# Attention over a cached window beside an MLP, one token: the value rows loaded in longer runs, and the product with them laid out anew

## The chip, the cores and the metric

The kernel runs on one core of one Trainium2 chip. The metric is the device time of one execution in microseconds (us). Before the change it is 99.78 us, the median of 3 runs from 99.64 to 99.85. A core has five engines with an instruction queue each: TensorE (PE, matrix products; its weight loads are listed as PEld), VectorE (DVE), ScalarE (ACT), GpSimd (POOL) and SyncE (SP), which here issues the loads. The loads of one queue are carried out by 16 DMA engines in the order in which they were issued.

## The reference

One token `x` of 1024 numbers is normalised to `xn`; an attention over the last 4096 cached keys and values and an MLP both start from `xn`, and their results are added to `x`:

```python
xn  = layernorm(x)
# A: 32 query heads of 128; 4 groups of keys and values, 8 heads on each; the last W = 4096 rows of 65536
q   = xn @ wq                                   # wq 1024 x 4096
p   = softmax(q . k[:, -W:] * 128 ** -0.5)
o   = p . v[:, -W:]
A   = o.reshape(4096) @ wo                      # wo 4096 x 1024
# B
h   = gelu(layernorm(xn) @ w1 + b1)             # w1 1024 x 3584
B   = h @ w2 + b2                               # w2 3584 x 1024
out = x + A + B
```

Everything is bf16. With one token there is no reuse: each of `wq`, `w1`, `w2`, `wo` and the two cache windows is read once, 39.86 MB in all.

## The kernel before

The kernel is a list of operations in the order of the source. Each `op(engine, ...)` names the tiles that it reads and writes; a small planner (`Plan.emit`) keeps the order of each engine as it is written and puts in the semaphore waits. So the order on an engine, and the order of the loads on SP's queue, are set by hand.

The loads go into four 4-MB buffers `slot[0]` to `slot[3]`, each used several times; a load into a slot waits for the last readers of what was there. In the order of SP's queue: the first row of `wq` (slot 1), the keys K (slot 0), the rest of `wq` (slots 1 and 2), the small biases, `w1` in two halves (slot 1, then slot 0), the values V (slot 2, once the second half of `wq` has been used), the first 14 rows of `w2` in two loads of 6 and 8 rows (slot 3, once the keys have been copied out of it), its last 14 rows (slot 1), the first 16 rows of `wo` in two loads (slot 0), and the last 16 in five (slot 2, once V has been used). A "row" of a weight is what each of the 128 partitions holds of it: partition p has 8 of `wq`'s rows, 28 of `w2`'s, 32 of `wo`'s, each 1024 numbers wide for `w2` and `wo`.

The stages that the change and the prediction touch:

- Keys (L341 to L350). K is loaded in runs of 32 KB: partition 4r + g holds 128 consecutive tokens of group g. DVE transposes it in blocks of 32 x 32 into slot 3, and ACT and DVE copy the blocks to `kT`.
- Scores (L417 to L431). PE multiplies `qm` with `kT` in 32 products of 512 columns, four at a time side by side, one for each of four token sets R; the four groups g are accumulated into one 128 x 1024 result: row 32R + head.
- Softmax (L433 to L467). Copy to `sc`, maximum, exponentials `e128` on ACT (L457) with their sums, transposed in blocks by DVE into `eTb` (L461). `rs` is one over the sum of a head; `grs` is that times the mask `gmask`, which keeps a head's own group.
- MLP. The first half of `w1`'s product (`w1_part(0)`) follows the scores on PE, the second the maximum. DVE adds the bias (`h_pre`, L471), ACT applies gelu (L473), DVE transposes (`hT`, L475). DVE adds 21 of `w2`'s 28 rows, each weighted with a number of its own per partition, into two running sums (`running`, L489, with L486 for the first of one sum); PE takes the other 7 (`PE_ROWS`).
- V's product (`v_step`, L502). 32 products, a first, fifteen turns of a loop of two, and a last one. Partition p of V holds 32 tokens of each group, as four runs of 8 KB; product c has the exponentials of token c for 32 heads as weights (and 96 surplus columns) and 4 x 128 columns of V, so its result has every head against every group. L518 masks it with `grs`, L520 adds the four groups, L522 rounds to `o_bf`.
- Output (L525 to L577). PE spreads `o_bf` to `o8` (four small products, L241), then takes `PE_ROWS` and `wo`'s rows: 16 one at a time, 8 in pairs (`groups=2`, two products side by side in the array), which DVE adds to its running sum (L557), and the last 8 rows apart, with the running sum summed over the partitions between them (products of `run` with `ones_f`). `res` is rounded by DVE and ACT and stored by two small DMAs.

Which loads the running rows and the products wait for is in their keys (`w200`, `w206`, `w21`, `wo00` and so on). The running sums on DVE stand in two batches, nine rows ahead of L518 and twelve behind L522.

## Time and profile before

| | |
|---|---|
| median of 3 runs | 99.78 us (99.64 to 99.85) |
| the profiled execution | 99.68 us, of which its span is 98.4 us |
| PE busy | 56.0 us, 323 products |
| DVE busy | 73.1 us |
| ACT busy | 30.8 us |
| POOL busy | 9.9 us |
| mean granted clock of TensorE | 0.931 |

The span is the time from the first to the last instruction in the hardware profiler's record; the 1.28 us that the execution takes beside it lie outside what the profile shows. Busy times overlap, since the engines run side by side. A wait is put down to what came last. A load's row gives the size of the load and the time from its issue to its landing, which includes the time that it stands behind earlier loads of its queue.

The costliest groups of instructions touched by the change, from the list of groups:

| line, engine | what | count, busy us |
|---|---|---|
| L489 DVE | a row of `w2` into a running sum | 20, 24.2 |
| L235 PE | rows of `wo` | 48, 9.1 |
| L502 PE | V's product | 32, 11.6 |
| L235 PE | scores | 32, 5.3 |
| L235 PE | `w2`'s rows on PE | 14, 3.2 |
| L475 DVE | transpose of `h_sb` | 1, 1.7 |
| L461 DVE | transpose of the exponentials | 1, 1.2 |
| L457 ACT | exponentials | 1, 1.2 |

### The profile page before, as it was taken

To read this page: it belongs to the slowest core of one execution; us is meant where nothing else is said; L and a number is where in the kernel's file an instruction comes from. 1 tells how busy PE (TensorE), PEld (TensorE's weight loads), DVE (VectorE), ACT (ScalarE), POOL (GpSimd) and SP (SyncE) were. 2 spreads that over 40 slices of the span, in tenths; PEclk is the share of its full clock that TensorE was granted. 3 is DMA by queue.
4 is the path that set the end of the run, shared out by engine and by line. 5 is a ranking of instruction groups with operands and counts; after the bars stand their busy time and mean duration, and the time that the engine had idled before them with its cause. 6 is when DMAs were issued, how large, how long until landed. Compare 5 with 4: busy or idle time off the path is not lost.

```text
span 98.4 us, 951 instructions
## 1 busy us (share of the span) xinstructions
PE 56.0 (57%) x323; PEld 16.0 (16%) x220; DVE 73.1 (74%) x75; ACT 30.8 (31%) x29; POOL 9.9 (10%) x22
## 2 busy tenths in 40 slices
PE   0140400699200699930899547977771839595792
PEld 0040000133000234300212211211210101111130
DVE  0146407999999999999005595999989999999231
ACT  0600000099999899992002193000000000000001
POOL 0626810000000670000000000000000000000000
PEclk9999999999996559999579998599999999999999
DMA  3999979999999899989799999999898999999980
GB/s 60 487 426 453 440 310 470 433 533 426 440 426 403 373 385 513 408 373 513 330 426 426 423 438 430 425 426 480 385 524 343 433 426 433 426 433 406 396 323 1
DMA packets 3084, 39.86 MB, mean 405 GB/s; under 512 B 390, under 2 KB 396, under 8 KB 780
## 3 DMA queue, kind: packets, MB, share of 16 engines
q1 hardware_dynamic: 3034, 39.86, 95.7%
q10 hardware_dynamic: 50, 0.00, 0.0%
HBM read 39.86 MB, written 0.00 MB: 405 GB/s over the span
## 4 chain that ended last, share of the span: by engine, by line
DMA 67%; PE 22%; issue 4%; SPq 2%; DVE 0%
DMA slot<-in_A_wq_dram 29%; DMA slot<-in_A_wo_dram 21%; DMA slot<-in_A_v_cache_dram 17%; PE qo_ps L502 12%; PE acc L376 9%; SPq L221 2%; PE acc L241 1%; DVE res L576 0%; PE acc L235 0%
## 5 line engine op out<-in xcount | busy, mean ns | idle before, releaser
L346 ACT COPY kT<-slot 32x1024 bf16<-32x1024 bf16 (+1 forms) x18 | 23.9, 1327 | 15.9 <-DVE slot L341 15.7
L489 DVE SCALAR_TENSOR_TENSOR run<-slot,hTf,run 128x1024 f32<-128x1024 bf16 x20 | 24.2, 1272 | 0.1
L376 PE MATMUL acc<-slot,xw 128*128 x48 | 15.4, 495 | 13.7 <-DMA slot<-in_A_wq_dram 13.7
L341 DVE STREAM_TRANSPOSE slot<-slot 128x4096 bf16<-128x4096 bf16 x4 | 17.4, 4414 | 3.6 <-DMA slot<-in_A_k_cache_dram 3.6
L502 PE MATMUL qo_ps<-slot,eTb 128*128 (+1 forms) x32 | 11.6, 437 | 4.3 <-issue 2.6
L350 DVE COPY kT<-slot 32x4096 bf16<-32x4096 bf16 x10 | 13.2, 1320 | 0.2
L235 PE MATMUL sc_ps<-slot,o 128*1 128x512 bf16 x48 | 9.1, 378 | 4.3 <-DMA slot<-in_A_wo_dram 4.3
L376 PEld LDWEIGHTS acc<-slot,xw 128*128 x48 | 5.5, 115 | 24.3 <-issue 21.9
L577 ACT CAST res<-acc 33x224 bf16<-33x224 f32 x1 | 0.3, 339 | 20.5 <-PE acc L235 20.5
L235 PE MATMUL sc_ps<-kT,qm 128*32 128x512 bf16 x32 | 5.3, 853 | 0.3 <-DVE qm L423 0.3
L502 PEld LDWEIGHTS qo_ps<-slot,eTb 128*128 (+1 forms) x32 | 3.1, 97 | 12.5 <-issue 9.8
L545 ACT CAST o<-misc 128x32 bf16<-128x32 f32 x1 | 0.2, 186 | 15.0 <-PE misc L241 15.0
L227 PEld LDWEIGHTS <-o 128*1 128x1 bf16 x40 | 2.4, 83 | 13.9 <-issue 13.3
L435 DVE COPY sc<-sc_ps 128x512 f32<-128x512 f32 x1 | 0.7, 691 | 4.9 <-PE sc_ps L235 4.9
L241 PE MATMUL acc<-spread,qm 32*128 32x512 bf16 x4 | 1.6, 498 | 3.7 <-POOL qm L322 3.7
L235 PE MATMUL sc_ps<-slot,hT 128*1 128x512 bf16 x14 | 3.2, 378 | 0.5 <-DMA slot<-in_B_w_dram 0.5
L235 PE MATMUL acc<-slot,yT 128*1 128x448 bf16 x64 | 3.4, 353 | 0.0
L434 ACT COPY sc<-sc_ps 128x512 f32<-128x512 f32 x1 | 0.6, 585 | 8.0 <-PE sc_ps L235 8.0
L241 PE MATMUL qo_ps<-selq,q_sb 128*128 128x4 bf16 x8 | 0.4, 166 | 4.3 <-DVE q_sb L395 4.3
L241 PE MATMUL misc<-x,spread 32*128 32x8 bf16 x4 | 0.3, 168 | 4.4 <-POOL spread L262 4.4
L557 DVE TENSOR_TENSOR run<-sc_ps,run 33x512 f32<-33x512 f32 x2 | 1.3, 678 | 1.8 <-PE sc_ps L235 1.8
L235 PE MATMUL acc<-slot,o 128*1 128x288 bf16 (+1 forms) x32 | 2.2, 272 | 0.7 <-DMA slot<-in_A_wo_dram 0.6
(88 smaller groups left out, 43.6 us busy)
## 6 DMA issues: line engine op xcount, KB each, us to landing
slot<-in_B_w_dram SPq DMA_DIRECT2D x3, 3584.0 KB, 16.7
slot<-in_A_wo_dram SPq DMA_DIRECT2D x3, 2048.0 KB, 23.7
slot<-in_A_k_cache_dram SPq DMA_DIRECT2D x1, 4096.0 KB, 14.0
slot<-in_A_wq_dram SPq DMA_DIRECT2D x1, 4096.0 KB, 28.6
slot<-in_A_v_cache_dram SPq DMA_DIRECT2D x1, 4096.0 KB, 16.8
slot<-in_A_wq_dram SPq DMA_DIRECT2D x2, 1024.0 KB, 9.8
slot<-in_A_wq_dram SPq DMA_DIRECT2D x1, 2048.0 KB, 19.3
slot<-in_B_w_dram SPq DMA_DIRECT2D x1, 2048.0 KB, 21.5
```

Of the source, the lines that this page charges most:

```text
L221: plan.add(eng, lambda: q.dma_start(out=out_ap, in_=in_ap), r, w, True, over)
L227: return pe.add_instruction(mybir.InstLdweights(name=nc.get_next_instruction_name(), engine=i.engine, tile_size=(P, 32), tile_position=pos ...
L235: return pe.add_instruction(mybir.InstMatmult(name=nc.get_next_instruction_name(), engine=i.engine, start_tensor_calc=start, stop_tensor_c ...
L241: op("pe", lambda: pe.matmul(out_ap, lhsT=w_ap, rhs=x_ap, start=start, stop=stop, tile_position=pos), r, w)
L341: op("dve", lambda s=s: dve.transpose(out=scr[:, s, :], in_=k2[:, s, :]), ("k", "slot0"), (f"scr{s}",))
L346: op("act", lambda s0=s0, s1=s1, R=R, Cd=Cd: act.copy(out=kT[32 * Cd:32 * Cd + 32, R, s0:s1, :].rearrange("p s (c j) -> p (s c) j", j=32), ...
L350: op("dve", lambda R=R, Cd=Cd: dve.tensor_copy(out=kT[32 * Cd:32 * Cd + 32, R, :, :].rearrange("p s (c j) -> p (s c) j", j=32), in_=T3[32 ...
L376: pe.matmul(acc2[:, b, :], lhsT=xw[:, bass.ds(32 * n + 512 * i, P)], rhs=slot[1 + i][:, bass.ds(1024 * n + 512 * b, 512)], start=False, st ...
L435: op("dve", lambda: dve.tensor_copy(out=sc[:, 0:512], in_=sc_ps[:, 0, :]), ("sc0",), ("scs0",))
L489: op("dve", lambda: dve.scalar_tensor_tensor(out=t, in0=wap, scalar=hTf[:, c:c + 1], in1=t, op0=ALU.mult, op1=ALU.add), (key, "hTf", f"run ...
L502: return pe.matmul(qo_ps, lhsT=cols, rhs=v4[:, :, c, :], start=first, stop=last)
L557: op("dve", lambda half=half: dve.tensor_tensor(out=run[0][0:33, 512 * half:512 * half + 512], in0=bulk[:, half, :], in1=run[0][0:33, 512 ...
```

## The change

- V is loaded in runs of 32 KB, as K is: partition 4r + g holds 128 consecutive tokens of group g. It goes into slot 3 and waits for the copies of the keys. The first 14 rows of `w2` go into slot 2, in one load instead of two, and are issued ahead of V. The last 16 rows of `wo` go into slot 3, behind V's product.
- The scores' rows are now 32g + 8u + h for group g, one of four tokens u and head h of the group. `qm` is a 128 x 4 x 4 x 32 tile with each group's heads at four places. The number and size of the products stay.
- The exponentials, transposed in blocks, are moved across partitions by two products with a permutation `perm` into PSUM (`e_ps`), so that they lie as V lies. ACT then writes them four times into `eM`, scaled with `own[:, g]`, which is 1 on the partitions that hold group g and 0 elsewhere (`own_heads`). One of the four stands ahead of the gelu on ACT, three behind it.
- V's product still has 32 steps of 512 columns. Step w has the exponentials of four tokens, 4 x 32 heads, as weights and the same four tokens of V as columns; of the 4 x 4 blocks of the result only the diagonal ones are wanted. DVE copies these four blocks out of PSUM and adds them; ACT rounds, and multiplies with `rs`.
- `gmask`, `grs` and the padding of `eTb` go. `perm` and `own` are made on DVE.
- DVE's batches of running rows are 16 ahead of V's blocks and 5 behind. On PE, `PE_ROWS` stand ahead of the spreading of `o_bf`; all 24 rows of `wo` that go through `bulk_rows` are taken in pairs.

```diff
+    e_ps = ps("e_ps", [P, NCH * 4, REP])
...
-    gmask = sb("gmask", [Hq, Hkv], FP32)
...
+    own = sb("own", [P, Hkv], FP32)
+    op("dve", lambda: dve.tensor_reduce(out=own, in_=ident_f.rearrange("p (r g) -> p g r", g=Hkv), axis=AX.X, op=ALU.add), ("ident_f",), ("own",))
+    perm = sb("perm", [P, P], BF16)
+    op("dve", lambda: dve.tensor_copy(out=perm.rearrange("p (r g) -> p r g", g=Hkv), in_=ident_f.rearrange("p (g r) -> p r g", g=Hkv)), ("ident_f",), ("perm",))
-    qm = sb("qm", [P, Hkv, Hq], BF16)
+    qm = sb("qm", [P, Hkv, 4, Hq], BF16)
...
-    dma("sp", v_sb.rearrange("p (g n) -> p g n", g=Hkv), A_v_cache[0, :, Sk - W:Sk, :].rearrange("g (p c) d -> p g (c d)", p=P), (), ("v0",), ("slot2",))
+    w2_t = [slot[i][:, :14 * D].rearrange("p (r n) -> p r n", r=14) for i in (2, 1)]
+    dma("sp", w2_t[0], w2_v[:, 0:14, :], (), ("w20",), ("slot2",))
+    v_sb = slot[3]
...
-    for a, b in ((0, 6), (6, 14)):
-        dma("sp", w2_t[0][:, a:b, :], w2_v[:, a:b, :], (), (f"w20{a}",), kt_srcs)
+    dma("sp", v_sb, A_v_cache[0, :, Sk - W:Sk, :].rearrange("g (r c) d -> r g (c d)", r=P // Hkv), (), ("v0",), kt_srcs)
     dma("sp", w2_t[1], w2_v[:, 14:28, :], (), ("w21",), ("slot1",))
...
+    for b in range(2):
+        mm32(e_ps[:, 64 * b:64 * b + 64, :], perm, eTb[:, 64 * b:64 * b + 64, :], True, True, ("perm", "eTb"), (f"e_ps{b}",))
...
+    eM = sb("eM", [P, NCH * 4, Hq], BF16)
+
+    def own_heads(g):
+        op("act", lambda: act.activation(out=eM[:, :, REP * g:REP * g + REP], in_=e_ps, func=ACT.Copy, scale=own[:, g:g + 1]),
+           ("e_ps0", "e_ps1", "own"), (f"eM{g}",))
...
+    own_heads(0)
     h_sb = sb("h_sb", [P, 2 * NH], BF16)
     op("act", lambda: act.activation(out=h_sb, in_=h_pre.rearrange("p b n -> p (b n)"), func=ACT.Gelu_apprx_tanh), ("h_pre",), ("h_sb",))
+    for g in (1, 2, 3):
+        own_heads(g)
...
-    for c in dve_rows[:9]:
+    for c in dve_rows[:16]:
         running(c)
...
-        cols = eTb[:, bass.ds(32 * c, P)] if not isinstance(c, int) else eTb[:, 32 * c:32 * c + P]
-        return pe.matmul(qo_ps, lhsT=cols, rhs=v4[:, :, c, :], start=first, stop=last)
+            cols, keys = eM_w[:, bass.ds(P * w, P)], v_sb[:, bass.ds(512 * w, 512)]
+        return pe.matmul(qo_ps, lhsT=cols, rhs=keys, start=first, stop=last)
...
-        dma("sp", wo_t[1][:, a:b, :], wo_v[:, 16 + a:16 + b, :], (), (f"wo1{a}",), ("slot2",))
-    o_m = sb("o_m", [Hq, Hkv, Dh], FP32)
-    op("dve", lambda: dve.tensor_tensor(out=o_m, in0=o_all.rearrange("h (g d) -> h g d", g=Hkv), in1=grs.unsqueeze(2).to_broadcast([Hq, Hkv, Dh]), op=ALU.mult), ("qo", "grs"), ("o_m",))
+        dma("sp", wo_t[1][:, a:b, :], wo_v[:, 16 + a:16 + b, :], (), (f"wo1{a}",), ("slot3",))
+    o_u = sb("o_u", [Hq, 4, Dh], FP32)
+    for u in range(4):
+        op("dve", lambda u=u: dve.tensor_copy(out=o_u[:, u, :], in_=qo_ps[32 * u:32 * u + 32, Dh * u:Dh * u + Dh]), ("qo",), (f"o_u{u}",))
...
-    op("dve", lambda: dve.tensor_copy(out=o_bf, in_=o_f), ("o_f",), ("o_bf",))
-    for c in dve_rows[9:]:
+    op("act", lambda: act.activation(out=o_bf, in_=o_f, func=ACT.Copy, scale=rs), ("o_f", "rs"), ("o_bf",))
+    for c in dve_rows[16:]:
         running(c)
...
+    bulk_rows(PE_ROWS, w2_row, hcol, "hT", first=True)
     o8_ps = misc[:, 160:192]
...
-    bulk_rows(PE_ROWS, w2_row, hcol, "hT", first=True)
...
-    bulk_rows(list(range(16)), wo_row, ocol, "o8")
-    bulk_rows(list(range(16, NB)), wo_row, ocol, "o8", last=True, groups=2)
+    bulk_rows(list(range(NB)), wo_row, ocol, "o8", last=True, groups=2)
```

More of the change, by code (lines that the diff above doesn't have):

```diff
@@ L271 @@
                                           pattern=[[32, 4]], channel_multiplier=1), ("selq",), ("selq",))
-    gmask = sb("gmask", [Hq, Hkv], FP32)
-    op("pool", lambda: pool.memset(gmask, 1.0), (), ("gmask",))
-    op("pool", lambda: pool.affine_select(out=gmask, in_=gmask, compare_op=ALU.is_ge, fill=0.0, base=0,
-                                          pattern=[[-REP, Hkv]], channel_multiplier=1), ("gmask",), ("gmask",))
-    op("pool", lambda: pool.affine_select(out=gmask, in_=gmask, compare_op=ALU.is_ge, fill=0.0, base=REP - 1,
-                                          pattern=[[REP, Hkv]], channel_multiplier=-1), ("gmask",), ("gmask",))
     ones_f = sb("ones_f", [P, P], FP32)
@@ L319 @@
     sel4 = sb("sel4", [P, Hq], FP32)
-    op("dve", lambda: dve.tensor_reduce(out=sel4, in_=ident_f.rearrange("p (r h) -> p h r", r=4), axis=AX.X, op=ALU.add), ("ident_f",), ("sel4",))
-    qm = sb("qm", [P, Hkv, Hq], BF16)
+    op("dve", lambda: dve.tensor_reduce(out=sel4.rearrange("p (g h) -> p g h", g=Hkv), in_=ident_f.rearrange("p (g u h) -> p g h u", g=Hkv, u=4),
+                                        axis=AX.X, op=ALU.add), ("ident_f",), ("sel4",))
+    own = sb("own", [P, Hkv], FP32)
[3 more added lines that the diff above has]
+    qm = sb("qm", [P, Hkv, 4, Hq], BF16)
     op("pool", lambda: pool.memset(qm, 0.0), (), ("qm",))
@@ L378, in wq_rows @@
         return rows
-    qz, zrow = qm.rearrange("p g h -> p (g h)")[0:Hq, :], spread.rearrange("p u n -> p (u n)")
+    qz, zrow = qm[0:Hq, 0, :, :].rearrange("p u h -> p (u h)"), spread.rearrange("p u n -> p (u n)")
     for b in range(2):
@@ L398 @@
     dma("sp", w1_t[1], w1_v[:, 4:8, :], (), ("w11",), ("slot0",))
-    v_sb = slot[2]
-    v4 = v_sb.rearrange("p (g c d) -> p g c d", g=Hkv, c=NCH)
-    dma("sp", v_sb.rearrange("p (g n) -> p g n", g=Hkv), A_v_cache[0, :, Sk - W:Sk, :].rearrange("g (p c) d -> p g (c d)", p=P), (), ("v0",), ("slot2",))
+    w2_t = [slot[i][:, :14 * D].rearrange("p (r n) -> p r n", r=14) for i in (2, 1)]
+    dma("sp", w2_t[0], w2_v[:, 0:14, :], (), ("w20",), ("slot2",))
+    v_sb = slot[3]
     def w1_part(i):
@@ L420 @@
             mm32(qT_ps[:, k, :], blk, selq, True, True, (f"q_sb{b}", "selq"), ("qo",))
-    qm_d = qm.rearrange("p g h -> p (g h)")
-    qm_d = bass.AP(tensor=qm_d.tensor, offset=qm_d.offset, ap=[list(qm_d.ap[0]), [Hq + REP, Hkv], [1, REP]])
-    op("dve", lambda: dve.tensor_copy(out=qm_d, in_=qT_ps.rearrange("p k g -> p g k")), ("qo",), ("qm",))
-    for g in range(Hkv):
-        for R in range(4):
-            ldw(qm[:, g, :], (0, 32 * R), ("qm",))
+    qm_d = bass.AP(tensor=qm.tensor, offset=qm.offset, ap=[list(qm.ap[0]), [4 * Hq, Hkv], [Hq + REP, 4], [1, REP]])
+    op("dve", lambda: dve.tensor_copy(out=qm_d, in_=qT_ps.rearrange("p k g -> p g k").unsqueeze(2).to_broadcast([P, Hkv, 4, REP])), ("qo",), ("qm",))
+    for u in range(4):
+        for g in range(Hkv):
+            ldw(qm[:, g, u, :], (0, 32 * g), ("qm",))
         for a in range(2):
-            for R in range(4):
-                kv = kT[:, R, :, :].rearrange("p u (b r h) -> p h b u r", r=8, h=Hkv)[:, g, 16 * a:16 * a + 16]
-                mm(sc_ps[32 * R:32 * R + 32, a, :].rearrange("p (b r u) -> p b u r", r=8, u=4), qm[:, g, :], kv,
-                   g == 0, g == Hkv - 1, (0, 32 * R), kt_keys, (f"sc{a}",))
+            for g in range(Hkv):
+                kv = kT.rearrange("p q s (w u r k) -> p k u (s w) q r", u=4, r=8, k=Hkv)[:, g, u, 16 * a:16 * a + 16, :, :]
+                mm(sc_ps[32 * g:32 * g + 32, a, :].rearrange("p (w q r) -> p w q r", q=4, r=8), qm[:, g, u, :], kv,
+                   u == 0, u == 3, (0, 32 * g), kt_keys, (f"sc{a}",))
     w1_part(0)
@@ L435 @@
     op("dve", lambda: dve.tensor_copy(out=sc[:, 0:512], in_=sc_ps[:, 0, :]), ("sc0",), ("scs0",))
-    w2_t = [slot[i][:, :14 * D].rearrange("p (r n) -> p r n", r=14) for i in (3, 1)]
-    for a, b in ((0, 6), (6, 14)):
-        dma("sp", w2_t[0][:, a:b, :], w2_v[:, a:b, :], (), (f"w20{a}",), kt_srcs)
+    dma("sp", v_sb, A_v_cache[0, :, Sk - W:Sk, :].rearrange("g (r c) d -> r g (c d)", r=P // Hkv), (), ("v0",), kt_srcs)
     dma("sp", w2_t[1], w2_v[:, 14:28, :], (), ("w21",), ("slot1",))
@@ L444 @@
     op("pe", lambda: pe.transpose(mT_ps, m_loc, ident_f), ("m_loc", "ident_f"), ("misc",))
-    m_row = sb("m_row", [1, Hq], FP32)
-    op("dve", lambda: dve.tensor_reduce(out=m_row, in_=mT_ps.rearrange("a (r h) -> a h r", r=4), axis=AX.X, op=ALU.max), ("misc",), ("m_row",))
-    m_rep = sb("m_rep", [1, 4, Hq], FP32)
-    op("dve", lambda: dve.tensor_copy(out=m_rep, in_=m_row.unsqueeze(1).to_broadcast([1, 4, Hq])), ("m_row",), ("m_rep",))
+    m_row = sb("m_row", [1, Hkv, REP], FP32)
+    op("dve", lambda: dve.tensor_reduce(out=m_row, in_=mT_ps.rearrange("a (g u h) -> a g h u", g=Hkv, u=4), axis=AX.X, op=ALU.max), ("misc",), ("m_row",))
+    m_rep = sb("m_rep", [1, Hkv, 4, REP], FP32)
+    op("dve", lambda: dve.tensor_copy(out=m_rep, in_=m_row.unsqueeze(2).to_broadcast([1, Hkv, 4, REP])), ("m_row",), ("m_rep",))
     mc_ps = misc[:, 128:129]
-    mm32(mc_ps, m_rep.rearrange("a r h -> a (r h)"), ones_f[0:1, 0:1], True, True, ("m_rep", "ones_f"), ("misc",))
+    mm32(mc_ps, m_rep.rearrange("a g u h -> a (g u h)"), ones_f[0:1, 0:1], True, True, ("m_rep", "ones_f"), ("misc",))
     w1_part(1)
@@ L458 @@
     op("act", lambda: act.activation(out=dummy[:, 1:2], in_=mhalf[0:1, 0:1], func=ACT.Gelu_apprx_tanh), ("mhalf",), ("act_warm",))
-    eTb = sb("eTb", [P, WQ4 + 96], BF16)
-    op("pool", lambda: pool.memset(eTb[:, WQ4:], 0.0), (), ("eTb_pad",))
-    op("dve", lambda: dve.transpose(out=eTb[:, :WQ4], in_=e128), ("e128",), ("eTb",))
+    eTb = sb("eTb", [P, NCH * 4, REP], BF16)
+    op("dve", lambda: dve.transpose(out=eTb.rearrange("p c h -> p (c h)"), in_=e128), ("e128",), ("eTb",))
+    for b in range(2):
+        mm32(e_ps[:, 64 * b:64 * b + 64, :], perm, eTb[:, 64 * b:64 * b + 64, :], True, True, ("perm", "eTb"), (f"e_ps{b}",))
     rs_ps = misc[0:Hq, 144:145]
@@ L465 @@
     op("dve", lambda: dve.reciprocal(out=rs, in_=rs_ps), ("misc",), ("rs",))
-    grs = sb("grs", [Hq, Hkv], FP32)
-    op("dve", lambda: dve.tensor_scalar_mul(out=grs, in0=gmask, scalar1=rs), ("gmask", "rs"), ("grs",))
+    eM = sb("eM", [P, NCH * 4, Hq], BF16)
+    def own_heads(g):
+        op("act", lambda: act.activation(out=eM[:, :, REP * g:REP * g + REP], in_=e_ps, func=ACT.Copy, scale=own[:, g:g + 1]),
+           ("e_ps0", "e_ps1", "own"), (f"eM{g}",))
     h_pre = sb("h_pre", [P, 2, NH], FP32)
     op("dve", lambda: dve.tensor_tensor(out=h_pre, in0=acc2[:, :, :NH], in1=b1x.rearrange("p (b n) -> p b n", b=2), op=ALU.add), ("acc2", "b1x"), ("h_pre",))
+    own_heads(0)
     h_sb = sb("h_sb", [P, 2 * NH], BF16)
     op("act", lambda: act.activation(out=h_sb, in_=h_pre.rearrange("p b n -> p (b n)"), func=ACT.Gelu_apprx_tanh), ("h_pre",), ("h_sb",))
+    for g in (1, 2, 3):
+        own_heads(g)
     hT = sb("hT", [P, CW2, 32], BF16)
@@ L480, in w2_row @@
         i, r = divmod(c, 14)
-        return w2_t[i][:, r, :], "w21" if i else f"w20{0 if r < 6 else 6}"
+        return w2_t[i][:, r, :], "w21" if i else "w20"
     def running(c):
@@ L492, with v_step @@
     dve_rows = [c for c in range(CW2) if c not in PE_ROWS]
-    for c in dve_rows[:9]:
+    for c in dve_rows[:16]:
         running(c)
-    o_all = qo_ps[0:Hq, :]
-    v_in = ("eTb", "eTb_pad", "v0", "slot2")
-    def v_step(c, first, last):
-        cols = eTb[:, bass.ds(32 * c, P)] if not isinstance(c, int) else eTb[:, 32 * c:32 * c + P]
-        return pe.matmul(qo_ps, lhsT=cols, rhs=v4[:, :, c, :], start=first, stop=last)
+    v_in = ("eM0", "eM1", "eM2", "eM3", "v0", "slot3")
+    eM_w = eM.rearrange("p c h -> p (c h)")
+    def v_step(w, first, last):
+        if isinstance(w, int):
+            cols, keys = eM_w[:, P * w:P * w + P], v_sb[:, 512 * w:512 * w + 512]
+        else:
+            cols, keys = eM_w[:, bass.ds(P * w, P)], v_sb[:, bass.ds(512 * w, 512)]
+        return pe.matmul(qo_ps, lhsT=cols, rhs=keys, start=first, stop=last)
     def v_rows(i):
@@ L510 @@
     op("pe", lambda: v_step(NCH - 1, False, True), v_in, ("qo",))
-    wo_t = [slot[s].rearrange("p (r n) -> p r n", r=16) for s in (0, 2)]
+    wo_t = [slot[s].rearrange("p (r n) -> p r n", r=16) for s in (0, 3)]
     for a in (0, 8):
@@ L515 @@
     for a, b in zip(cuts[:-1], cuts[1:]):
-        dma("sp", wo_t[1][:, a:b, :], wo_v[:, 16 + a:16 + b, :], (), (f"wo1{a}",), ("slot2",))
-    o_m = sb("o_m", [Hq, Hkv, Dh], FP32)
-    op("dve", lambda: dve.tensor_tensor(out=o_m, in0=o_all.rearrange("h (g d) -> h g d", g=Hkv), in1=grs.unsqueeze(2).to_broadcast([Hq, Hkv, Dh]), op=ALU.mult), ("qo", "grs"), ("o_m",))
+        dma("sp", wo_t[1][:, a:b, :], wo_v[:, 16 + a:16 + b, :], (), (f"wo1{a}",), ("slot3",))
+    o_u = sb("o_u", [Hq, 4, Dh], FP32)
+    for u in range(4):
+        op("dve", lambda u=u: dve.tensor_copy(out=o_u[:, u, :], in_=qo_ps[32 * u:32 * u + 32, Dh * u:Dh * u + Dh]), ("qo",), (f"o_u{u}",))
     o_f = sb("o_f", [Hq, Dh], FP32)
-    op("dve", lambda: dve.tensor_reduce(out=o_f, in_=o_m.rearrange("h g d -> h d g"), axis=AX.X, op=ALU.add), ("o_m",), ("o_f",))
+    op("dve", lambda: dve.tensor_reduce(out=o_f, in_=o_u.rearrange("h u d -> h d u"), axis=AX.X, op=ALU.add), ("o_u0", "o_u1", "o_u2", "o_u3"), ("o_f",))
     o_bf = sb("o_bf", [Hq, Dh], BF16)
-    op("dve", lambda: dve.tensor_copy(out=o_bf, in_=o_f), ("o_f",), ("o_bf",))
-    for c in dve_rows[9:]:
+    op("act", lambda: act.activation(out=o_bf, in_=o_f, func=ACT.Copy, scale=rs), ("o_f", "rs"), ("o_bf",))
+    for c in dve_rows[16:]:
         running(c)
```

## The prediction, made before the changed kernel was run

> **What bounds the kernel now.** I read the page's DMA part first, then the rows of the loads one by one, then TensorE's and VectorE's rows in order of time.

> ```profile
> DMA  3999979999999899989799999999898999999980
> DMA packets 3084, 39.86 MB, mean 405 GB/s; under 512 B 390, under 2 KB 396, under 8 KB 780
> q1 hardware_dynamic: 3034, 39.86, 95.7%
> ```

> SP's queue keeps the 16 DMA engines busy 95.7% of the span; only the first slice and the last one and a half are empty. So it is not an engine that sets the time, but how long the packets take, plus a head and a tail. Rows of single loads (KB, us from issue to landing), and below them their issues (start us, us):

> ```profile
> slot<-in_A_wq_dram SPq DMA_DIRECT2D x1, 1024.0 KB, 4.8
> slot<-in_A_k_cache_dram SPq DMA_DIRECT2D x1, 4096.0 KB, 14.0
> slot<-in_B_w_dram SPq DMA_DIRECT2D x1, 3584.0 KB, 16.7
> slot<-in_A_v_cache_dram SPq DMA_DIRECT2D x1, 4096.0 KB, 16.8
> slot<-in_B_w_dram SPq DMA_DIRECT2D x1, 2048.0 KB, 21.5
> ```

> ```profile
> 0.80 0.40 SPq L207 DMA_DIRECT2D slot<-in_A_wq_dram  x1
> 1.26 0.64 SPq L207 DMA_DIRECT2D slot<-in_A_k_cache_dram  x1
> 32.73 0.33 SPq L221 DMA_DIRECT2D slot<-in_B_w_dram  x1
> 42.60 0.38 SPq L221 DMA_DIRECT2D slot<-in_A_v_cache_dram  x1
> 46.46 0.45 SPq L221 DMA_DIRECT2D slot<-in_B_w_dram  x1
> ```

> Issue plus latency is the landing, and a load's own time is its landing less that of the load ahead of it. K, runs of 32 KB: 1.26 + 14.0 = 15.26, behind a first row of wq at 0.80 + 4.8 = 5.6: 9.7 us. V, the same 4 MB in runs of 8 KB: 42.60 + 16.8 = 59.4, behind w1 at 32.73 + 16.7 = 49.4: 9.95 us. The landings in the trace have a digit more: 5.55, 15.25, 49.43, 59.37, so 9.70 and 9.94. The packet records say the same: 311 ns on average for an 8-KB packet of V, 1214 ns for a 32-KB packet of K, that is 30 ns less than four of 8 KB.

> ```profile
> 59.51 1.03 PE L502 MATMUL qo_ps<-slot,eTb 128*128 128x512 bf16 x3 [1.72 <-DMA slot<-in_A_v_cache_dram]
> 72.73 0.94 PE L502 MATMUL qo_ps<-slot,eTb 128*128 x3 [0.26 <-issue]
> 76.51 3.18 PE L235 MATMUL sc_ps<-slot,hT 128*1 128x512 bf16 x14 [0.52 <-DMA slot<-in_B_w_dram]
> 91.18 1.89 PE L235 MATMUL sc_ps<-slot,o 128*1 128x512 bf16 x16 [1.28 <-DMA slot<-in_A_wo_dram]
> 93.67 1.03 PE L235 MATMUL acc<-slot,o 128*1 128x288 bf16 x16 [0.60 <-DMA slot<-in_A_wo_dram]
> 65.00 8.45 DVE L489 SCALAR_TENSOR_TENSOR run<-slot,hTf,run 128x1024 f32<-128x1024 bf16 x7
> 90.05 1.23 DVE L525 TENSOR_TENSOR run<-run 128x1024 f32<-128x1024 f32 x1
> 93.11 1.28 DVE L557 TENSOR_TENSOR run<-sc_ps,run 33x512 f32<-33x512 f32 x2 [1.83 <-PE sc_ps L235]
> ```

> PE waits for a landing ahead of every stage (V, w2's end, wo's pieces), DVE for PE at the end. From w1's landing on, each load lands as soon as its bytes allow. The last lands at 96.23; 2.17 us of products, rounding and stores end the span.

> **The change, part by part.** *V's runs.* 512 packets become 128. K has this very layout (partition 4r + g) and size, so V's load should take 9.70 us in place of 9.94: -0.24. Bounds: nothing, if V keeps its present rate; -0.25 by the packet records (512 x 311 / 16 against 128 x 1214 / 16). I take K's row.

> [...]

> *w2's first 14 rows in one load.* Its two loads landed at 63.06 and 67.96, 8.58 us behind V. The same 3.5 MB as one load of 28-KB runs is w21: 67.96 to 76.46, 8.50. So -0.08 (bounds 0 and -0.08), and SP has one issue fewer.

> *The order on SP.* The load into slot 2 waits as V's did (42.60), the one into slot 3 as w2's did (46.09); no wait is new. The engines start on them at 49 and later, so both are early, and w21's issue, queued behind, still waits for PE until 54.3. V now lands 8.50 later less 0.24: 49.43 + 8.50 + 9.70 = 67.63. w20 lands at 57.93.

> *wo's last 16 rows wait for V's product.* In the rows it runs from 59.51 to 73.69: 14.18 us for 32 steps, and it has 32 steps of 512 columns still, with as many register instructions in the loop. So 67.78 to 81.96. Queued behind V stand w21 and wo's first 16 rows; their packets are through near 85.5 (86.25, the landing now, less 0.32 and less the 0.4 from last packet to landing), and then the DMA engines run dry. First packets follow an issue by 1.0 us (0.80 to 1.82 at the start), so the product may end at 84.5: 2.5 us to spare. Without that cover every us of lateness is a us of the total.

> *Exponentials.* eTb is ready at 58.80. Two permuting products of 512 columns take 0.60 (the pair at L241), the small one of the sums follows at 59.7, the reciprocal queued behind it ends at 59.9, and h_pre, queued behind that on DVE, ends at 61.0 in place of 60.1. A mask of 1024 numbers per partition costs 1.15, by the exponentials' own row (bounds 1.0, from the 512-wide PSUM copy of 0.585, and 1.9, the 2048-wide key copy). The first is over by 60.7, so gelu waits for h_pre alone; three more end at 65.4 (67.7 at 1.9 each): V comes at 67.63. All of this lies under V's load. For qm's copy, four times as wide (0.19 now), I add 0.1; the scores' 32 products, of the same shapes with other strides, I leave at 5.29, and allow 0.5 either way. Running rows so start 1.0 later, at 64.1.

> *DVE.* Its first nine rows took 10.32 us (63.13 to 73.45), a further row 1.204 (8.45 / 7 in the row above, 14.42 / 12 later). Sixteen end at 64.1 + 10.32 + 7 x 1.204 = 82.85, after V's product. Four block copies from PSUM at 0.29 (between 0.19 for 32 columns and 0.69 for 512) and the sum, 1.00: 85.0. Five rows, 6.02, and L525's add, 1.23: 92.25 in place of 91.28. It is needed when the bulk products end, at 93.1 less what the loads gain, 92.8: 0.55 to spare, the thinnest margin.

> *PE.* PE_ROWS (3.18) follow V's product at once, to 85.15; o_bf is there at 85.25, o8 at 85.9, and wo's second 8 rows land at 86.25 - 0.32 = 85.93. Sixteen rows in pairs at 1.89 per eight end at 89.7, the next 8 land at 90.8. 1.1 to spare; one at a time (3.61 per eight) they would not fit, so the pairs pay for the later start.

> *Set-up.* own and perm on DVE (under 0.73 each, as sel4's row) fall into its 3.6 us of waiting for K; without that they would cost 1 us. POOL drops gmask's three and makes qm four times as large (+0.3 at most, as spread's 0.51); the products behind it wait for wq until 18.1 anyway.

> Sum: -0.24 - 0.08 = -0.32, all of it in the loads. 99.68 - 0.32 = 99.36 for an execution like the profiled one, which lies 0.10 under the median; for the median, 99.46.

> **The rivals.** *Run length gives nothing in this place:* V at its present rate. For it, the rate from landing to landing hardly changes anywhere (K 4.19 MB in 9.70, V in 9.94 us); against it, three sizes of run stand in order (wq's second half, 32 KB, also takes 9.73, with the small biases among it). 99.7 to 99.8, within 0.2%.

> *DVE comes last.* Place: the add of L525 and the sums behind it. It decides from 0.55 us on. For it, DVE has no gap from 64 to 92, and everything added ahead of h_pre or between the rows lands in that chain. With block copies at the upper row of 0.69 (+1.6) and scores slower by 0.5, it is 2.1 late, 1.55 beyond the margin: 101.0; with half of that 100.0. Against it, the narrow PSUM copy's 0.19 is nearer in size than the wide one.

> *The clock falls to half in the last stage.* PE idles from about 60 to 67.6. These windows show what V's product does then (us, PE busy, clock, DMA share, GB/s):

> ```profile
> 60.85:64.30 3.45, 3.45 (x8) 0.51 1.07 454
> 64.30:73.70 9.40, 7.04 (x22) 1.00 1.03 443
> ```

> Eight steps in 3.45 at half clock, 22 in 9.40 at full: 0.43 us a step both times, so a cold start costs it nothing. The pairs leave idle time at 89.7 to 90.8; should the clock halve for 3.4 us behind that, the last 24 products and the 16 behind them would lose about 1.5: 101.0. Against it, the stretches of 3.4 us from 74.5 and 84.8 were busy for 49% and 62% and the clock stayed at full speed; it fell behind the one from 57.44, at 42%, and mine are never below 60%. [...]

> **How the numbers follow.** The forecast 0.68; run length worthless 0.10; DVE last 0.12; the clock 0.06; anything else late, V's product above all, 0.04. The forecast's own range is 99.3 to 99.65. A measurement tells about 0.2% here, 0.2 us. Faster than 99.58: 0.63, nearly all of the forecast. Within: the rest of it, the first rival, a slight lateness of DVE, 0.18. Slower: 0.19. The range goes from 99.25, a faster median by the spread of the runs, to 100.2, the milder half of the late cases.

> **What would show it.** V's load between landings 9.7 us, w2's first load 8.5; the DMA engines without a gap until the last load, 0.3 earlier; V's product starting at its landing, not at a mask; wo's last rows issued near 82; DVE waiting for PE, if briefly, ahead of the final sums. Wrong would make it: a gap between wo's halves in the DMA slices, PE waiting for DVE ahead of the products of run, or V at 9.9.

## The result, and the profile after

The change makes the kernel slower: 102.84 us, the median of 6 runs from 102.74 to 104.08, against 99.86 (99.64 to 100.68); the ratio is 1.031, with a 95% interval from 1.026 to 1.036. The forecast was 99.46 in a range from 99.25 to 100.2.

But the span became shorter. In the other executions of the changed kernel it is 98.1 to 98.3 us, where the kernel before has 98.3 to 98.7. In the profiled one it is 99.2, since one of the 16 DMA engines fell 0.9 us behind while K was loaded (fifteen of K's 16 parts had landed by 15.26, the last at 16.15), and the loads behind it wait for it as well (fifteen parts of V by 67.63, the last at 68.49). What grew is the part of the execution beside the span: 1.28 us before (99.68 - 98.40), 4.6 to 5.0 now (102.79 - 98.2 and its like). Here is the DMA view of the changed kernel from 98.5 to 106 us, in 40 slices of 0.19 us:

```profile
DMA  0000000000000000040000000000000000000000
q8 instruction: 1, 0.02, 1.1%
```

and the same view of the kernel before from 98 us on:

```profile
DMA packets 0, 0.00 MB, mean 0 GB/s; under 512 B 0, under 2 KB 0, under 8 KB 0
```

2.6 us after the last instruction of the changed kernel has ended, at slice 17 (101.7 us), one packet of 16 KB is loaded that isn't data but instructions. It takes 1.37 us by its record. If the 104.08 us of this execution are counted from the start of the span, it ends 1.0 us behind the packet. The page shows nothing of it: it stops at the span.

Within the span, the page's DMA part and the rows of the loads answer to those of before:

```profile
DMA  3999979999999899899899899999899999999960
q1 hardware_dynamic: 2506, 39.86, 95.1%
slot<-in_B_w_dram SPq DMA_DIRECT2D x1, 3584.0 KB, 16.6
33.63 0.33 SPq L222 DMA_DIRECT2D slot<-in_B_w_dram  x1
slot<-in_B_w_dram SPq DMA_DIRECT2D x1, 3584.0 KB, 15.3
43.43 0.33 SPq L222 DMA_DIRECT2D slot<-in_B_w_dram  x1
slot<-in_A_v_cache_dram SPq DMA_DIRECT2D x1, 4096.0 KB, 21.5
46.95 0.59 SPq L222 DMA_DIRECT2D slot<-in_A_v_cache_dram  x1
```

w1's second half lands at 50.2, w2's first 14 rows at 58.7, V at 68.5. In the trace's digits: 50.27, 58.78, 68.49, so 8.51 us for w2's rows (8.58 before) and 9.72 for V (9.94). The DMA engines have no gap until the end. TensorE and VectorE, in order of time:

```profile
68.63 6.62 PE L506 MATMUL qo_ps<-slot,eM 128*128 128x512 bf16 x15 [9.41 <-DMA slot<-in_A_v_cache_dram]
81.89 0.89 PE L506 MATMUL qo_ps<-slot,eM 128*128 x3 [0.30 <-issue]
86.37 3.62 PE L236 MATMUL sc_ps<-slot,o 128*1 128x512 bf16 x32 [0.28 <-ACT o L551]
92.02 1.89 PE L236 MATMUL sc_ps<-slot,o 128*1 128x512 bf16 x16 [2.04 <-DMA slot<-in_A_wo_dram]
82.82 1.18 DVE L523 COPY o_u<-qo_ps 32x128 f32<-32x128 f32 x4 [0.75 <-PE qo_ps L506]
91.07 1.23 DVE L530 TENSOR_TENSOR run<-run 128x1024 f32<-128x1024 f32 x1
93.95 1.28 DVE L560 TENSOR_TENSOR run<-sc_ps,run 33x512 f32<-33x512 f32 x2 [1.66 <-PE sc_ps L236]
```

V's product starts at V's landing, wo's pairs wait 2.0 us for their last rows, and VectorE waits 1.7 us ahead of the final sums. Everything that the prediction hid is hidden. The loss is all outside the span.

### The profile page after: what moved, and what is told of

Same layout as the page of the kernel before. It is cut to its first block, busy times and chain, and to the rows that moved or that the text cites. A ratio compares the mean times of both kernels' runs of the same rounds, so it can differ in the third digit from the quotient of the medians.

```text
span 99.2 us, 956 instructions
## 1 busy us (share of the span) xinstructions
PE 51.4 (52%) x324; PEld 15.0 (15%) x222; DVE 74.6 (75%) x78; ACT 35.3 (36%) x34; POOL 8.7 (9%) x18
## 2 busy tenths in 40 slices
DMA packets 2556, 39.86 MB, mean 402 GB/s; under 512 B 374, under 2 KB 380, under 8 KB 764
## 3 DMA queue, kind: packets, MB, share of 16 engines
q1 hardware_dynamic: 2506, 39.86, 95.1%
HBM read 39.86 MB, written 0.00 MB: 402 GB/s over the span
## 4 chain that ended last, share of the span: by engine, by line
DMA 48%; DVE 31%; PE 15%; issue 3%; SPq 1%
DMA slot<-in_A_v_cache_dram 22%; DVE slot L340 18%; DMA slot<-in_A_k_cache_dram 15%; DVE kT L349 13%; PE qo_ps L506 12%; DMA slot<-in_A_wo_dram 11%; PE acc L236 2%; PE acc L242 1%; DVE res L579 0%; SPq L208 0%; SPq L222 0%
## 5 line engine op out<-in xcount | busy, mean ns | idle before, releaser
L345 ACT COPY kT<-slot 32x1024 bf16<-32x1024 bf16 (+1 forms) x18 | 23.9, 1327 | 16.8 <-DVE slot L340 16.6
L506 PE MATMUL qo_ps<-slot,eM 128*128 (+1 forms) x32 | 12.0, 480 | 11.6 <-DMA slot<-in_A_v_cache_dram 9.4
L236 PE MATMUL sc_ps<-slot,o 128*1 128x512 bf16 x48 | 5.5, 378 | 2.3 <-DMA slot<-in_A_wo_dram 2.0
L506 PEld LDWEIGHTS qo_ps<-slot,eM 128*128 (+1 forms) x32 | 3.2, 99 | 20.2 <-issue 18.1
L465 ACT ACTIVATE eM<-e_ps,own 128x1024 bf16<-128x1024 f32 x4 | 4.2, 1108 | 0.5 <-PE e_ps L242 0.5
L236 PE MATMUL sc_ps<-kT,qm 128*32 128x512 bf16 x32 | 3.9, 647 | 0.4 <-DVE qm L420 0.4
L228 PEld LDWEIGHTS <-o 128*1 128x1 bf16 x40 | 1.7, 83 | 8.4 <-issue 7.3
L311 DVE TENSOR_SCALAR yT<-xn,st 128x8 bf16<-128x8 f32 x1 | 2.1, 2135 | 0.7 <-POOL st L309 0.7
## 6 DMA issues: line engine op xcount, KB each, us to landing
slot<-in_B_w_dram SPq DMA_DIRECT2D x4, 3584.0 KB, 16.2
slot<-in_A_wo_dram SPq DMA_DIRECT2D x3, 2048.0 KB, 24.7
slot<-in_A_k_cache_dram SPq DMA_DIRECT2D x1, 4096.0 KB, 14.9
slot<-in_A_wq_dram SPq DMA_DIRECT2D x1, 4096.0 KB, 29.5
slot<-in_A_v_cache_dram SPq DMA_DIRECT2D x1, 4096.0 KB, 21.5
slot<-in_A_wq_dram SPq DMA_DIRECT2D x2, 1024.0 KB, 10.2
slot<-in_A_wq_dram SPq DMA_DIRECT2D x1, 2048.0 KB, 20.2
slot<-in_A_wo_dram SPq DMA_DIRECT2D x1, 1024.0 KB, 11.3
```

The source lines that it names most:

```text
L228: return pe.add_instruction(mybir.InstLdweights(name=nc.get_next_instruction_name(), engine=i.engine, tile_size=(P, 32), tile_position=pos ...
L236: return pe.add_instruction(mybir.InstMatmult(name=nc.get_next_instruction_name(), engine=i.engine, start_tensor_calc=start, stop_tensor_c ...
L311: op("dve", lambda: dve.tensor_scalar(out=yT, in0=xn, scalar1=st12[:, 2:3], scalar2=st12[:, 6:7], op0=ALU.subtract, op1=ALU.mult), ("xn", ...
L345: op("act", lambda s0=s0, s1=s1, R=R, Cd=Cd: act.copy(out=kT[32 * Cd:32 * Cd + 32, R, s0:s1, :].rearrange("p s (c j) -> p (s c) j", j=32), ...
L465: op("act", lambda: act.activation(out=eM[:, :, REP * g:REP * g + REP], in_=e_ps, func=ACT.Copy, scale=own[:, g:g + 1]), ("e_ps0", "e_ps1" ...
L506: return pe.matmul(qo_ps, lhsT=cols, rhs=keys, start=first, stop=last)
```

## The experiments

What could bring such a fetch is the length of the programs, that is, the number of an engine's instructions, a loop's counted once. TensorE's has 451 instructions before and 455 after: the two permuting products, each with its weight load. ScalarE's went from 53 to 58, VectorE's from 104 to 106, GpSimd's and SyncE's got shorter. All times below are medians beside runs of the kernel before on the same chip; "outside" is the time less the span, as the median over the runs.

**Four instructions more on TensorE alone, or seven on the others.**

```diff
+    for b in range(2):
+        mm32(acc2[:, b, :], qz, zrow, False, False, ("qm", "spread"), ("acc2",))
```

> The kernel before, with two products of zeros more on TensorE at the start (two weight loads and two products, 451 to 455 instructions in TensorE's program, as in the changed kernel); the other engines' programs as before, and TensorE waits for wq there anyway. Theory 'length of TensorE's program': the loss of the change lies outside the span, in a fetch of 16 KB of instructions after the last one, because the program got four instructions longer; this kernel then takes about 103.1 (99.8 + 3.3) with its span at 98.4 as before. Rival 'something in the change's work': 99.8. Rival 'ScalarE's or VectorE's program': 99.8.

103.03 against 99.82, ratio 1.033 (1.029 to 1.038), span 98.55 as before. The profile, from 98.2 us on, shows the packet again, at 100.4 us:

```profile
q8 instruction: 1, 0.02, 0.9%
```

On the other engines (the first line five times, the second twice):

```diff
+    op("act", lambda: act.activation(out=dummy[:, 0:1], in_=mhalf[0:1, 0:1], func=ACT.Exp), ("mhalf",), ("act_warm",))
+    op("dve", lambda: dve.memset(ones_f, 1.0), (), ("ones_f",))
```

> The kernel before, with five tiny activations more on ScalarE and two memsets more on VectorE at the start (53 to 58 and 104 to 106 instructions, as in the changed kernel), TensorE's program unchanged at 451. Theory 'length of TensorE's program': 99.8, span 98.4. Rival 'ScalarE's or VectorE's program': about 103.1.

99.84 against 99.82, ratio 1.000 (0.996 to 1.004), no such packet. The whole loss of the change comes with four instructions on TensorE that do nothing, so it is neither the change's work nor the other engines' programs.

**Two and three more.** One product of zeros as above (453), and with it `ldw(xw[:, 96:97], (0, 0), ("xw",))` (454).

> The kernel before with one product of zeros more on TensorE at the start: 453 instructions in its program, between 451 (nothing fetched at the end) and 455 (3.2 us lost). Theory 'a block boundary in TensorE's program': all or nothing, 99.8 or about 103.1, by whether the end has crossed the boundary, which this run brackets. Rival 'each instruction more costs': about 101.4.

> The kernel before with one product of zeros and one weight load more: 454 instructions on TensorE, between 453 (no fetch) and 455 (3.2 us lost). Theory 'a block boundary': all or nothing, 99.8 or about 103.

453: 99.81 against 99.77, outside 1.31, no packet. 454: 100.15 against 99.74, ratio 1.006 (1.002 to 1.011), outside 1.66 against 1.31, no packet in the record. So neither a cost for each instruction nor quite all or nothing: 0, 0.35, 3.2 us at 453, 454, 455. Where the 0.35 come from isn't settled.

**The change with two and four instructions less.** The maximum of the scores is kept in bf16 (453), then the first sum of x goes through a bf16 product too (451):

```diff
-    m_loc = sb("m_loc", [P, 1], FP32)
+    m_loc = sb("m_loc", [P, 1], BF16)
...
-    op("pe", lambda: pe.transpose(mT_ps, m_loc, ident_f), ("m_loc", "ident_f"), ("misc",))
+    mm32(mT_ps, m_loc, perm, True, True, ("m_loc", "perm"), ("misc",))
...
-    m_rep = sb("m_rep", [1, Hkv, 4, REP], FP32)
+    m_rep = sb("m_rep", [1, Hkv, 4, REP], BF16)
...
-    mm32(mc_ps, m_rep.rearrange("a g u h -> a (g u h)"), ones_f[0:1, 0:1], True, True, ("m_rep", "ones_f"), ("misc",))
+    mm32(mc_ps, m_rep.rearrange("a g u h -> a (g u h)"), spread[0:1, 0, 0:1], True, True, ("m_rep", "spread"), ("misc",))
...
-    mm32(tot, ones_f, st[:, 0:1], True, True, ("ones_f", "st0"), ("misc",))
+    mm32(tot, ones_b, sum_b, True, True, ("ones_b", "st0"), ("misc",))
```

> The changed kernel with the scores' maximum kept in bf16, which makes one fp32 product into a bf16 one and saves two instructions: 453 in TensorE's program. The same work otherwise, and a maximum that is rounded alike in exponent and sum changes nothing in the softmax. Theory 'a block boundary': the same answer as the kernel before at 453, so 99.6 if that took 99.8, or 102.9 if that took 103.1. Rival 'something in the change's work': 102.8 whatever the other does.

> As the one ahead, and the first sum of x through a bf16 product as well, two instructions less: 451 in TensorE's program, as many as the kernel before has. All loads, masks, V's product and wo's pairs as in the changed kernel. Theory 'a block boundary': no fetch at the end, 99.55 (99.8 less 0.25 of the shorter span), faster than both kernels. Rival 'something in the change's work': 102.8.

453: 99.55 against 99.77, ratio 0.9966 (0.9940 to 0.9993). 451: 99.54, ratio 0.9971 (0.9939 to 1.0004). Spans 98.2, outside 1.3 in both, no packet of 16 KB. With all of the change's loads, masks and products in it, the version of 453 is faster than both kernels, by what the prediction saw in the loads or a little less; that of 451 is faster by as much, though its interval just takes in 1.

**448 instructions, in two ways.** First the loop over the second half of wq with one unit a turn:

```diff
-    op("pe", lambda: pe_loop("wq1", 8, wq_rows(1, 2)), ("xw", "wq4", "slot2"), ("acc2",))
+    op("pe", lambda: pe_loop("wq1", 16, wq_rows(1, 1)), ("xw", "wq4", "slot2"), ("acc2",))
```

> The changed kernel with the loop over the second half of wq taking one unit a turn, 16 turns, instead of two a turn, 8 turns: the same products, TensorE's program 448 instructions instead of 455. Theory 'length of TensorE's program': the 3.3 us outside the span go, 99.6, if the longer loop (some 3 us more by the first loop's 0.77 a turn against 1.16) stays hidden behind the copies of the keys; span 98.2 or a little more. Rival 'something in the change's work': 102.8 or more.

100.22 (99.44 to 100.69) against 99.82, ratio 1.003 (0.999 to 1.007), outside 1.26. The 3.3 us are gone, but the spans scatter from 98.2 to 99.4, and a 16-KB packet is there, at 98.24, just before the last instruction ends at 98.27. Then 448 without that loop, the version of 451 with `PE_ROWS = list(range(22, 28))`:

> The changed kernel at 451 instructions, with one of w2's rows moved from TensorE to VectorE: 448 in TensorE's program, without the loop of 16 turns of the other kernel of 448 (100.2 us, with a fetch just at the end of its span). If a length of 448 brings the fetch, it is there again; if the 16 turns brought it, there is none and the time is 99.55, or up to 0.6 more if VectorE's row of 1.2 us no longer fits ahead of the final sums (it had 0.55 to spare by the prediction, 1.0 to 1.6 by the profiles).

99.58 against 99.74, ratio 0.998 (0.995 to 1.001), no packet. The short length isn't what brings the early packet; why the kernel of 16 turns has it stays open.

**The branch hints out, and a program much longer.**

```diff
-            back = self.engines[e].mark_branch_hint_location()
...
-            self.engines[e].br_eq(never[e], 1, f"{e}_main", f"{e}_last").branch_hint(back)
+            self.engines[e].br_eq(never[e], 1, f"{e}_main", f"{e}_last")
```

> The changed kernel with the branch hints of VectorE and TensorE taken out, which name the branch that stands at the end of both programs and its target at their start; 454 instructions on TensorE. If the hints decide which block of instructions is fetched ahead, the block that the end needs is fetched while the program runs: no fetch behind the span, 99.6. If they don't, the fetch stays behind the span: 102.8.

100.97 against 99.77, ratio 1.011 (1.004 to 1.018): outside 1.31, and nothing is fetched behind the span, but the span is 99.65. A 16-KB packet runs at 53.0 us and one of 8 KB at 66.9. Without the hints a packet of 16 KB is fetched at another time. The edit also takes one instruction from TensorE (454); but the kernel before at 454, with its hints, keeps its span (98.45 in the median, 98.4 without the three instructions more), so the hints are the likelier cause, though no run of the changed kernel with 454 instructions and its hints parts the two. The forecast of 99.6 overlooked what a fetch costs in the midst of the loads: w2's first load took 9.77 us instead of 8.51. The same is seen in the kernel before with sixteen products of zeros more (`for b in range(16)`, 483 instructions):

> The kernel before with sixteen products of zeros more on TensorE at the start, under its wait for wq: 483 instructions in its program. If one block boundary near the end is what costs, being 28 instructions further past it than the program of 455 still costs a fetch behind the span, about 3 us: 103. If only a narrow stretch of lengths around 455 is bad, or the block is fetched early enough once the boundary lies well ahead of the end, 99.8 to 101.2.

101.2 against 99.87, ratio 1.011 (1.009 to 1.014); outside 1.31, span 99.8. Its DMA view from 50 to 53 us, and w1's second half and V as loads and as issues:

```profile
q8 instruction: 1, 0.02, 2.2%
slot<-in_B_w_dram SPq DMA_DIRECT2D x1, 3584.0 KB, 16.7
32.75 0.33 SPq L221 DMA_DIRECT2D slot<-in_B_w_dram  x1
slot<-in_A_v_cache_dram SPq DMA_DIRECT2D x1, 4096.0 KB, 18.2
42.51 0.38 SPq L221 DMA_DIRECT2D slot<-in_A_v_cache_dram  x1
```

V lands 11.3 us behind w1 (60.7 less 49.4) instead of 9.94, and all later loads stay as late: the packet, 1.05 us long, goes through one of the 16 engines, each load is shared out over all 16, and the landing waits for the one that was held up. In the trace fifteen of V's 16 parts land from 59.03 to 59.33, the last at 60.75.

Behind the span of the same execution stands a second packet of 16 KB. The DMA view from 98 us on:

```profile
DMA  0000000000000004000000000000000000000000
q8 instruction: 1, 0.02, 1.0%
```

It runs from 101.06 to 102.38, and this execution took 102.08 us, 2.28 beside its span; the other four had 1.23 to 1.31. Counted from the start of the span, the packet ends 0.3 us after the execution. So a packet behind the span doesn't always bring 3.2 us, and here the end did not wait for it.

**V's runs alone,** in the kernel before:

```diff
-    dma("sp", v_sb.rearrange("p (g n) -> p g n", g=Hkv), A_v_cache[0, :, Sk - W:Sk, :].rearrange("g (p c) d -> p g (c d)", p=P), (), ("v0",), ("slot2",))
+    dma("sp", v_sb, A_v_cache[0, :, Sk - W:Sk, :].rearrange("g (r c) d -> r g (c d)", r=P // Hkv), (), ("v0",), ("slot2",))
```

> The kernel before, with V loaded in runs of 32 KB into the same slot at the same place in the queue and nothing else changed, so the tokens that a product meets are not those of its weights and the output isn't the reference's. Theory of the prediction (packet length): V's load 9.70 us between landings instead of 9.94, 99.55 in all, ratio 0.9975. Rival 'run length gives nothing in this place': ratio 1.000.

99.66 against 99.82, ratio 0.9964 (0.9932 to 0.9996); V's load 9.71 us (49.40 to 59.11). The first term of the sum holds as it stands.

**Without the pairs,** the version of 453 with wo's first 16 rows one at a time:

```diff
-    bulk_rows(list(range(NB)), wo_row, ocol, "o8", last=True, groups=2)
+    bulk_rows(list(range(16)), wo_row, ocol, "o8")
+    bulk_rows(list(range(16, NB)), wo_row, ocol, "o8", last=True, groups=2)
```

> The changed kernel at 453 instructions of TensorE, with wo's first 16 rows one at a time as in the kernel before, only the next 8 in pairs. The prediction's step: one at a time they take 7.2 us instead of 3.6 and end at about 92.7, 1.8 after the next rows land at 90.9; the final sums and all behind them come that much later, less what little the tail can take up: 101.0, span 99.7, TensorE without a gap ahead of the last pairs. Rival 'the pairs are hidden': 99.55.

101.09 against 99.74, ratio 1.013 (1.005 to 1.021), span 99.4:

```profile
85.56 8.15 PE L236 MATMUL sc_ps<-slot,o 128*1 128x512 bf16 x45 [0.28 <-ACT o L551]
```

TensorE has no gap ahead of the last pairs, where the changed kernel waits 2.04 us. In the spans the pairs are worth 1.2 us (99.4 against 98.2); the rest of the 1.5 us by which this version is slower than 99.55 lies outside them (1.8 in the median of four executions), and nothing here shows why.

## Why the prediction was wrong

The step that failed is the frame of the sum, "99.68 - 0.32 = 99.36 for an execution like the profiled one". It takes over the 1.28 us beside the span as a constant, and it costs the permuting products as "0.60" us of a hidden engine and nothing else. In its place the runs showed that four more instructions on TensorE, the change's own or products of zeros, add 3.2 us outside the span, and both traces of such kernels have a fetch of 16 KB of instructions behind it. None of the rivals had this; the rest "anything else late" had 0.04.

That the end of the execution waits for this fetch is argued: a packet starts behind the span at 455 instructions, and none does at 448 to 454. But the packets are only 1.37 and 1.17 us long; in the 2.6 and 1.9 us between the last instruction and them the traces show no work of the kernel; and the execution of the kernel of 483 ended before its second packet did. So what fills the 3.2 us stays open.

The cost of the fetch was not hidden here: 3.2 us came with it behind the span (455 instructions), 1.3 us with one within it (483).

Of the length that brings the fetch the runs show this much: behind the span there is none at 451 and 453 instructions, and one at 455. That a boundary between blocks of instructions lies there, as the expectations have it, was the author's estimate; no run shows such a boundary, and all or nothing it isn't. Nor do the runs show what brings the 0.35 us at 454, the early packet of the kernel with 16 turns and the second packet at 483.

Point by point:

- *V's runs*, -0.24: 9.72 against 9.94, -0.22 (in the kernel before, alone, -0.23). *w2's load*, -0.08: 8.51 against 8.58. The spans fell by 0.3 in the median, 98.5 to 98.2, the version of 453 by 0.22 in the time. Both terms held. A figure beside them is off by a hundredth: the packet records give a bound of -0.24, not -0.25.
- *V's product* from 67.78 for 14.18 us: from 68.63 for 14.15, the shift being this execution's late DMA engine. Its half clock at the start (0.50 from 68.63 to 74.70, before from 60.85 to 64.27) cost nothing, as said.
- *Exponentials*: a mask took 1.11 (1.15 said). The running rows started 0.25 later than before, not 1.0, although the late engine had cost them 0.9: the scores, which I left at 5.29, took 3.92. In the version of 453, without a late engine, the rows started 0.77 earlier than before (62.36 against 63.13).
- *VectorE's margin* of 0.55 was 1.66 (1.5 in the versions of 453 and 451), for that reason; the four copies took 1.18 (1.16), and a whole row of w2 more on VectorE still fitted (99.58 with 448 instructions). *TensorE's margin* of 1.1 was 2.0, and without the pairs the version of 453 went from 99.55 to 101.09 (101.0 expected), of which the span shows 1.2.
- *The clock* stayed full from the end of V's product on (1.00 from 82.78 to the end of the span). The rivals of run length, of VectorE last and of the clock all fall.

## What to carry to other kernels

Put the time of an execution beside its span, before and after: what lies outside is no constant, and a view that ends with the span can't show it. It varies within one kernel too: of 24 executions of the kernel before on one chip, 16 had 1.24 to 1.48 us outside and eight 1.97 to 2.72, so medians are compared. Where a change adds instructions, count the engine's whole program too; here 453 instructions on TensorE were free, 455 cost 3%, and an fp32 product made into a bf16 one gave the two back. In the kernel of 483 instructions, whose loads keep the 16 DMA engines busy 94.5% of the span, a single foreign packet of 1.05 us on one of them delayed the later landings by 1.3 to 1.4 us.

## What the runs showed of the hardware that was not expected

```profile
47.70 3.94 PE L236 MATMUL sc_ps<-kT,qm 128*32 128x512 bf16 x32 [0.39 <-DVE qm L424]
```

```profile
47.60 6.05 PE L235 MATMUL sc_ps<-kT,qm 128*32 128x512 bf16 x32 [0.29 <-DVE qm L424]
```
